# GpSimd left with 64-bit integer additions alone; its float work on VectorE, sums transposed inside PSUM, and a newly planned order

## The chip, the cores and the metric

The kernel runs on one core of one Trainium2 chip. The time is device microseconds from start to end of one launch. The unchanged kernel took 651.06 us (median of three runs, 650.86 to 653.36).

Engine names are those of the profile: PE is TensorE (PEld its weight loads), DVE is VectorE, ACT is ScalarE, POOL is GpSimd, SP is SyncE, which only issues DMAs here.

## The reference

Two attention blocks over separate inputs, S = 2048 tokens, D = 512, 32 heads of 16, bfloat16. Block A is linear attention, block B is full softmax attention. The output holds both side by side.

```python
def _A_ref(x, wqkv, wo):
    ...
    phi = lambda t: jnp.where(t > 0, t + 1, jnp.exp(t)) + 1e-6
    pq, pk = phi(q), phi(k)
    kv = jnp.einsum("bhsd,bhse->bhde", pk, v)
    z = jnp.einsum("bhsd->bhd", pk)
    num = jnp.einsum("bhqd,bhde->bhqe", pq, kv)
    den = jnp.einsum("bhqd,bhd->bhq", pq, z)[..., None] + 1e-6
    o = num / den
    ...
def _B_ref(x, wqkv, wo):
    ...
    scores = jnp.einsum("bhqd,bhkd->bhqk", q, k) * scale
    p = _softmax(scores, axis=-1)
    o = jnp.einsum("bhqk,bhkd->bhqd", p, v)
    return ... @ wo
```

Nearly all the work is in block B: 32 heads x 2048 x 2048 scores, each of which needs an exponential.

## The kernel before, in words

**Blocks and units.** The scores are cut into 2048 blocks of 128 keys x 512 queries of one head. Sixty-four blocks (four heads, which sit on the four 32-row groups `g` of PE, 16 key tiles `j`) make a unit, so there are 32 units `u` = (head group `Gp`, 512 queries `c`, parity `e_`). The products Q K of a block are one matmul (`qk`, L901). Its exponentials P then go into one or three matmuls with V (L1284), which add up in the one PSUM bank `pPV`, four heads on four row groups. The seventeenth column of V is 1.0, so the same matmul gives the sum of the exponentials.

**Two ways to an exponential.** A block goes one of two ways:

- *On ACT* (L1113): two or three blocks, 1024 or 1536 columns, are read from the PSUM tensor `pS` by one `Exp` and written as fp16 to a ring of 25 buffers `PT`. One matmul with V follows per block.
- *On DVE* (L1017, "D blocks"): one `tensor_scalar` reads 512 columns from `pD` (or a spare bank of `pS`) and writes `score*ESC + EB` as int16 into `DI`. The bits of that integer, read as fp16, are a rough exponential. Two more copies of the pattern are made by adding the integers 328 and 656 (`SHIFT`), and three matmuls with V, the first with a scaled V called `VX`, average the three approximations.

**The pattern copies.** Two D blocks (1024 columns) make a group, and there are eight group buffers in `DI`. In the kernel before, POOL makes the two copies as one int32 `tensor_tensor` addition (two int16 values in each 32-bit word, L1208), with up to four copies in one instruction. When POOL is behind, the second copy goes to DVE instead (L1171). POOL also has float work: `VX = VV * 1.55` (L714), the division of a finished unit by its sums (L1319), and a few small ones (L680, L697 to L699).

**The end of a unit.** When `pPV` is complete, DVE transposes it in 32x32 tiles into SBUF (L1313), which frees the bank for the next unit's matmuls. Then come the reciprocal of the sums (L1318, DVE), the product (L1319, POOL) and, after every second unit, a transposition back (L1324, DVE). `last_unit` does the same for the last unit in two halves (L1374 to L1379), and the output projection, the copies to bfloat16 and the stores follow (L1336, L597, L1389).

**What sets the order.** Each engine runs its own list in order. The lists are written by a planner in the kernel's own code: it keeps an estimated clock per engine, estimated durations for every operation and a table `SEG` of weights for each 12 us, and takes the best candidate each time. So a changed duration or weight gives another list on every engine, another choice of which blocks go to ACT and which to DVE, and other merges on POOL. `Sched.add` turns the reads and writes of each operation into semaphore waits. Other work (block A, the projections of block B) is put between as jobs with due times: `bjobs` for block B and for the flag below, `ajobs` for block A.

**The flag.** Row and column norms (`gram_x`, `gram_w`, `flag_job`) tell whether the scores are small enough for this way of taking exponentials. The flag is read at the very end, and a general version in the same program runs only if it is set, which it is not for these inputs.

## Time and profile before

| | |
|---|---|
| median of three runs | 651.06 us |
| profiled execution | 651.69 us |
| span from its first to its last instruction | 649.9 us |
| ACT busy | 633.5 us, 97% |
| PE busy | 637.8 us, 98% |
| DVE busy | 622.5 us, 96% |
| POOL busy | 616.8 us, 95% |
| granted TensorE clock | 0.999 |

The profile describes one execution. A row of a group has the line, engine and operation, what is written from what, the shape and count, then the busy time of the whole group, the mean of one instruction in ns, and the idle time just before them with what ended it. On ACT and DVE one instruction starts before the last has quite ended, so the busy time of a group is less than its count times the mean. A busy share says nothing by itself about which engine sets the end.

### The profile page before, as it was taken

How to read it: one execution, taken by the hardware profiler on the slowest of the kernel's cores; microseconds unless marked ns; L12 is line 12 of the kernel's file. 1: busy time of each engine (PE TensorE's matmuls, PEld its weight loads, DVE VectorE, ACT ScalarE, POOL GpSimd, SP SyncE). 2: the span in 40 equal slices, each digit the busy share in tenths (PEclk: the TensorE clock that was granted, in tenths of full speed). 3: DMA queues.
4: the chain of work that ended last, by engine and by line, in shares of the span. 5: the costliest groups of instructions: out<-in, count | busy, mean ns of one | idle time of the engine just before them, and what ended most of it. 6: DMA issues, size and time to landing. Idle time of an engine off the chain costs nothing.

```text
span 649.9 us, 19218 instructions
## 1 busy us (share of the span) xinstructions
PE 637.8 (98%) x8355; PEld 214.4 (33%) x8356; DVE 622.5 (96%) x1080; ACT 633.5 (97%) x689; POOL 616.8 (95%) x347
## 2 busy tenths in 40 slices
PE   8999999999999999999999999999999999999996
PEld 5333333332333334332232323332223332223332
DVE  4999999999999999999999999999999999999974
ACT  5999999999999999999999999999999999999994
POOL 5899999999999999999999999999999999999950
PEclk9999999999999999999999999999999999999999
DMA  9701000211100110200220200011000001100212
GB/s 171 220 2 24 12 1 10 43 24 29 16 20 2 34 34 2 40 9 7 48 69 2 49 26 19 2 34 42 24 13 22 3 2 42 34 18 17 50 50 69
DMA packets 53224, 21.73 MB, mean 33 GB/s; under 512 B 44176, under 2 KB 52624, under 8 KB 53136
## 3 DMA queue, kind: packets, MB, share of 16 engines
q1 hardware_dynamic: 51664, 19.80, 13.3%
q8 instruction: 67, 1.10, 0.7%
q10 hardware_dynamic: 1472, 0.66, 0.4%
q14 instruction: 21, 0.17, 0.1%
HBM read 4.46 MB, written 4.19 MB: 13 GB/s over the span
## 4 chain that ended last, share of the span: by engine, by line
ACT 66%; PE 16%; DVE 16%; DMA 1%; issue 0%; SPq 0%
ACT PT L1113 65%; DVE DI L1017 11%; PE pPV L1284 5%; PE pS L901 5%; PE pD L611 2%; ACT EA L723 1%; PE pS L611 1%; DVE DI L1171 1%; DMA xTb<-in_B_x_dram 1%; DVE PQT L726 1%; DVE VNa L813 1%; DVE KNa L597 0%; DVE OT L1313 0%; PE pS L1336 0%; PE pD L901 0%; DMA KNa<-VNa 0%
## 5 line engine op out<-in xcount | busy, mean ns | idle before, releaser
L1113 ACT ACTIVATE PT<-pS 128x1024 f16<-128x1024 f32 (+1 forms) x651 | 619.4, 1096 | 1.9 <-PE pS L901 1.0
L1208 POOL TENSOR_TENSOR DI<-DI,CW 128x1024 int32<-128x1024 int32 (+2 forms) x264 | 580.7, 2232 | 5.8 <-DVE DI L1017 4.3
L1017 DVE TENSOR_SCALAR DI<-pD 128x512 int16<-128x512 f32 x512 | 336.9, 682 | 5.7 <-PE pD L901 3.9
L901 PE MATMUL pS<-QT,KM 32*128 32x512 bf16 x1532 | 259.5, 384 | 2.9 <-ACT PT L1113 2.0
L1284 PE MATMUL pPV<-PT,VV 128*17 128x512 f16 x1338 | 232.6, 381 | 0.0
L1284 PE MATMUL pPV<-DI,VV 128*17 128x512 f16 x1420 | 232.0, 382 | 0.1
L901 PE MATMUL pD<-QT,KM 32*128 32x512 bf16 x516 | 185.7, 384 | 0.5 <-DVE DI L1017 0.4
L1284 PE MATMUL pPV<-DI,VX 128*17 128x512 f16 x710 | 162.8, 381 | 0.4 <-DVE OT L1313 0.4
L901 PEld LDWEIGHTS pS<-QT,KM 32*128 32x128 bf16 x1532 | 65.1, 91 | 238.9 <-ACT PT L1113 190.6
L1017 DVE TENSOR_SCALAR DI<-pS 128x512 int16<-128x512 f32 x194 | 131.5, 678 | 0.3 <-PE pS L901 0.3
L1284 PEld LDWEIGHTS pPV<-PT,VV 128*17 128x17 bf16 x1338 | 52.2, 88 | 42.4 <-issue 32.4
L1284 PEld LDWEIGHTS pPV<-DI,VV 128*17 128x17 bf16 x1420 | 49.5, 88 | 45.0 <-issue 33.6
L1171 DVE TENSOR_SCALAR DI<-DI 128x1056 int16<-128x1056 int16 x73 | 49.8, 687 | 0.2
L901 PEld LDWEIGHTS pD<-QT,KM 32*128 32x128 bf16 x516 | 44.2, 91 | 7.6 <-DVE DI L1017 5.2
L1284 PEld LDWEIGHTS pPV<-DI,VX 128*17 128x17 bf16 x710 | 35.6, 88 | 21.8 <-issue 15.7
L611 PE MATMUL pD<-Wa,xTa 128*32 128x256 bf16 x640 | 26.3, 275 | 0.1
L611 PE MATMUL pD<-xTb,Wb 128*32 128x512 bf16 x288 | 23.2, 384 | 0.0
L1313 DVE STREAM_TRANSPOSE OT<-pPV 128x512 f32<-128x512 f32 x31 | 21.9, 706 | 0.0
L1319 POOL TENSOR_TENSOR OT<-OT,ZR 128x256 bf16<-128x256 f32 x31 | 19.3, 621 | 1.1 <-DVE ZR L1318 1.0
L611 PEld LDWEIGHTS pD<-Wa,xTa 128*32 128x32 bf16 x640 | 14.0, 96 | 10.3 <-issue 6.1
L597 DVE CAST KNa<-pD 128x512 bf16<-128x512 f32 x21 | 14.3, 681 | 3.1 <-PE pD L611 3.1
L714 POOL TENSOR_SCALAR VX<-VV 128x544 bf16<-128x544 bf16 x16 | 10.2, 646 | 6.5 <-DVE VV L711 6.5
(139 smaller groups left out, 381.5 us busy)
## 6 DMA issues: line engine op xcount, KB each, us to landing
out_dram<-KNa SPq DMA_DIRECT2D x31, 128.0 KB, 1.7
Wa<-in_A_wqkv_dram SPq DMA_DIRECT2D x1, 1536.0 KB, 8.0
KM<-KR SPq DMA_DIRECT2D x96, 16.0 KB, 1.8
Wb<-in_B_wqkv_dram SPq DMA_DIRECT2D x2, 384.0 KB, 5.7
Wb<-in_B_wqkv_dram SPq DMA_DIRECT2D x1, 512.0 KB, 4.7
Wa<-in_A_wo_dram SPq DMA_DIRECT2D x1, 512.0 KB, 4.3
Wa<-in_B_wo_dram SPq DMA_DIRECT2D x1, 512.0 KB, 3.8
ON<-in_B_x_dram ACTq DMA_DIRECT2D x1, 256.0 KB, 2.9
```

Source lines behind the costliest of these rows:

```text
L597: return lambda e, bk: (e.tensor_copy(out_fn(), in_fn(bk)) if lane == "dve" else e.activation(out_fn(), in_fn(bk), ACTF.Copy))
L611: ins = self.e.matmul(out_[32 * g:32 * g + 32], lhsT=lhsT[:, 32 * g:32 * g + 32], rhs=rhs, start=start, stop=stop, tile_position=(0, 32 * g))
L714: st.append(("pool", 0.61, f_op("pool", lambda e: e.tensor_scalar(VX[:, r, 4 * t4:4 * t4 + 4, :].rearrange("p t c -> p (t c)"), VV[:, r, 4 ...
L723: ("act", 0.0635 + n * 0.000833, f_ev("act", lambda e, bk: e.activation(EA[:, 0:n], f32v(bk)[:, c0:c0 + n], ACTF.Exp), [], ["EA"])),
L901: return e.matmul(dst, lhsT=KM[32 * g:32 * g + 32, Gp % 2, e_, j * 128:(j + 1) * 128], rhs=QT[32 * g:32 * g + 32, Gp % 2, c * 512:(c + 1) ...
L1017: sch.add("dve", lambda e: e.tensor_scalar(DI[:, di_at(0, buf) + i * 512:di_at(0, buf) + (i + n) * 512], f32v(DBANK[b0], n * 512), ESC, EB ...
L1113: sch.add("act", lambda e: e.activation(PTf[:, p0 * 512:p0 * 512 + w], S5[:, c0:c0 + w], ACTF.Exp, scale=SC), reads=skeys(sl, len(bl)), wr ...
L1171: sch.add("dve", lambda e: e.tensor_scalar(gapped(DI, di_at(2, buf), wide // 32, 32), DI[:, di_at(0, buf) - 32:di_at(0, buf) + w], 1.0, fl ...
L1208: sch.add("pool", lambda e: e.tensor_tensor(dv, sv, cv, op=ALU.add), reads=keys + ["CW"], writes=[("DI", v, x) for v in vs for x in best])
L1284: sch.add("pe", lambda e, g=g, j=j, c0=c0, V_=V_, r2=r2, P=P, first=first, last_=last_: e.matmul(PVb[32 * g:32 * g + 17, 0:512] if len(P.s ...
L1313: sch.add("dve", lambda e: e.transpose(OT[:, 0, :], PVb[:, 0:512]), reads=[("PV", g) for g in range(4)], writes=[("OT", 0)])
L1319: ("pool", 0.59, f_op("pool", lambda e: e.tensor_tensor(xn[:, :, 16 * e_:16 * e_ + 16], o[:, :, 0:16], zr.unsqueeze(2).broadcast_to([128, ...
```

## The change

What it does, step by step:

1. **Copies.** Every pattern copy is one `int64_add` on POOL: four int16 values in a 64-bit word, plus a constant that holds 328 or 656 four times. There is one instruction per copy of a group (1024 int16 columns), never both copies in one. None goes to DVE any more; L1171 is gone, and with it its padded place in `DI`, so all rows for the matmuls are contiguous.
2. **Float work.** `VX` (16 instructions), the product of a unit (31 and the two halves of the last), the mask of `gram_w` and the three products of the flag go from POOL to DVE.
3. **End of a unit.** The transposition writes back into `pPV` itself. Reciprocal and product read the bank, so it is free for the next unit only after the product. The queries of Q are stored so that neighbouring ones of two 32-tiles form pairs; the transposition back then moves 4-byte pairs, 256 columns in place of 512.
4. **Start.** POOL writes the ones of V earlier, clears one `DI` pattern and runs one small `int64_add` on it at about its fifteenth instruction. Ahead of that first `int64_add` the built program has an instruction that loads other code for POOL (an `ISA` of line 526).
5. **Order.** New `SEG`, new durations for POOL (`PFX`, `PEL`), other due times: the Q and K projections of later head groups are spread, and the flag's jobs are due from 60 us instead of last.

In the program that results, 721 blocks go to DVE and 1327 to ACT, where there were 710 and 1338. ACT has 615 `Exp` of 1024 columns, 32 of 1536 and one of 512 (before: 615, 36 and none), and 32 of block A as before. DVE's evictions of D blocks are 703 of 512 columns and 9 of 1024 (before: 702 and 4).

The lines of the changed file are shifted: L901 is L912 there, L1017 is L1028, L1113 is L1124, L1284 is L1282, L1313 is L1311, L1318 is L1320, and the product is L1316. L1208 is the copy on POOL in both.

**POOL, around the product of the third unit, before** (sizes of `DI` are in 32-bit words, so 512 words are one copy of a group, 1024 both copies; OT is the product):

```order
L1208 TENSOR_TENSOR DI<-DI,CW 128x1024 x3
L1208 TENSOR_TENSOR DI<-DI,CW 128x512
L1319 TENSOR_TENSOR OT<-OT,ZR 128x16x16
L1208 TENSOR_TENSOR DI<-DI,CW 128x1024 x2
L1208 TENSOR_TENSOR DI<-DI,CW 128x2x512
L1208 TENSOR_TENSOR DI<-DI,CW 128x1024 x2
L1208 TENSOR_TENSOR DI<-DI,CW 128x512
```

The same engine from there to the end, changed:

```order
L1208 ISA DI<-DI 128x512 x30
L1208 ISA DI<-DI 128x2x512 x4
L1208 ISA DI<-DI 128x512 x250
L1208 ISA DI<-DI 128x256 x2
L1208 ISA DI<-DI 128x512 x86
L1208 ISA DI<-DI 128x256 x2
L1208 ISA DI<-DI 128x512 x344
L1208 ISA DI<-DI 128x256 x2
```

The list has become one kind of instruction, 720 of them where there were 264 larger ones, with nothing between.

**DVE, at the end of the seventh unit, before** (from the transposition to the reciprocal; DI from pD or pS are evictions of D blocks, KR a projection of K):

```order
L1313 STREAM_TRANSPOSE OT<-pPV 128x512
L1017 TENSOR_SCALAR DI<-pS 128x512
L1017 TENSOR_SCALAR DI<-pD 128x512
L649 CAST KR<-pD 128x512
L1017 TENSOR_SCALAR DI<-pS 128x512
L1017 TENSOR_SCALAR DI<-pD 128x512 x2
L1017 TENSOR_SCALAR DI<-pS 128x512
L1017 TENSOR_SCALAR DI<-pD 128x512
L1318 RECIPROCAL ZR<-OT 128x16
```

The same place, changed:

```order
L1311 STREAM_TRANSPOSE pPV<-pPV 128x512
L1028 TENSOR_SCALAR DI<-pS 128x512
L1028 TENSOR_SCALAR DI<-pD 128x512
L777 CAST VNa<-pD 128x4x128
L1028 TENSOR_SCALAR DI<-pS 128x512
L1028 TENSOR_SCALAR DI<-pD 128x512
L1320 RECIPROCAL ZR<-pPV 128x16
L1316 TENSOR_TENSOR OT<-pPV,ZR 128x8x2x16
```

Other work still stands between transposition and reciprocal, but now `pPV` is held until the last row. Over the 31 units there are 3.5 such instructions on average between the transposition and the product (0 to 10).

**PE, its last rows, before** (pPV matmuls of the last unit, then the output projection, `Wa` with `ON` and `xTb`):

```order
L1284 MATMUL pPV<-PT,VV 17x512 x12
L611 MATMUL pD<-Wa,ON 32x512 x12
L611 MATMUL pD<-Wa,xTb 32x512 x4
L1336 MATMUL pD<-Wa,ON 128x512 x3
L1336 MATMUL pS<-Wa,ON 128x512 x3
L1336 MATMUL pD<-Wa,xTb 128x512
L1336 MATMUL pS<-Wa,ON 128x512 x3
L1336 MATMUL pS<-Wa,xTb 128x512
L1336 MATMUL pS<-Wa,ON 128x512 x2
L1336 MATMUL pS<-Wa,xTb 128x512
L1336 MATMUL pS<-Wa,ON 128x512
L1336 MATMUL pS<-Wa,xTb 128x512
```

Changed:

```order
L1282 MATMUL pPV<-PT,VV 17x512 x7
L1336 MATMUL pS<-Wa,ON 128x512 x6
L1336 MATMUL pD<-Wa,xTb 128x512 x2
L1336 MATMUL pS<-Wa,xTb 128x512 x2
```

The sixteen L611 matmuls and six of the `ON` ones have gone to earlier places; the four `xTb` ones, which need the last transposition, now stand together at the end.

The diff, cut to its core:

```diff
-    PW = 0.4
+    PW = 0.5
...
-    TEND = 660.0
+    TEND = 632.0
...
-    PFX = 0.144
+    PFX = 0.173
+    PEL = 0.00041
...
-        DI = sb("DI", [128, NDG * (32 + 2 * DGW + (DGW // 32) * 33 + 32)], I16)
-        DIR = 32 + 2 * DGW + (DGW // 32) * 33 + 32
+        DIR = 3 * DGW
+        DI = sb("DI", [128, NDG * DIR], I16)
...
-        DW = DI.bitcast(mybir.dt.int32)
+        DW = DI.bitcast(mybir.dt.uint64)
...
+        sch.add("pool", lambda e: e.memset(DI[:, 0:DGW], 0.0), writes=[("DI", 0, 0, 0)])
+        sch.add("pool", lambda e: e.int64_add(DW[:, 0:8], DW[:, 8:16], 0), reads=[("DI", 0, 0, 0)], writes=[("DI", 0, 0, 0)])
...
+        def paired(ap):
+            return ap.rearrange("p (m t a) -> p m a t", t=32, a=2)
+        def in_pairs(ap):
+            return ap.rearrange("p (m a t) -> p m a t", t=32, a=2)
...
-                st.append(("dve", 0.6, f_ev("dve", lambda e, bk: e.tensor_copy(QT[:, r, cs], f32v(bk)), [], [("QT", r, sc)])))
+                st.append(("dve", 0.6, f_ev("dve", lambda e, bk: e.tensor_copy(in_pairs(QT[:, r, cs]), paired(f32v(bk))), [], [("QT", r, sc)])))
...
-            st.append(("pool", 0.61, f_op("pool", lambda e: e.tensor_scalar(
-                VX[:, r, 4 * t4:4 * t4 + 4, :].rearrange("p t c -> p (t c)"), VV[:, r, 4 * t4:4 * t4 + 4, :].rearrange("p t c -> p (t c)"),
+            st.append(("dve", 0.37, f_op("dve", lambda e: e.tensor_scalar(
+                gapped(VX[:, r, t4, :], 0, 33, 17), VV[:, r, t4, :],
...
-            def on_dve(st_, en_):
-                wide = w + 32
-                sch.add("dve", lambda e: e.tensor_scalar(gapped(DI, di_at(2, buf), wide // 32, 32), DI[:, di_at(0, buf) - 32:di_at(0, buf) + w], 1.0, float(SHIFT[1]),
-                                                         op0=ALU.mult, op1=ALU.add), reads=rk, writes=[("DI", 2, buf)])
-                give(buf, 2, "dve", en_)
...
-                sch.add("pool", lambda e: e.tensor_tensor(dv, sv, cv, op=ALU.add), reads=keys + ["CW"], writes=[("DI", v, x) for v in vs for x in best])
+                for v in vs:
+                    word = int.from_bytes(struct.pack("<4H", *[SHIFT[v - 1]] * 4), "little")
+                    sch.add("pool", lambda e, v=v, word=word: e.int64_add(at64(v), at64(0), word), reads=keys, writes=[("DI", v, x) for x in best])
+                    T["pool"] = st_ = st_ + PFX + len(best) * w * PEL
...
-            if p_backlog(s_["t"]) - DSH * d_backlog(s_["t"]) > PSH:
-                vs = (1,)
-                push("dve", s_["t"], 1, 0.06 + (w + 32) * 0.00053, on_dve)
...
-            sch.add("dve", lambda e: e.transpose(OT[:, 0, :], PVb[:, 0:512]), reads=[("PV", g) for g in range(4)], writes=[("OT", 0)])
-            pvopen[0] = t_ + LPE["dve"]
...
+            sch.add("dve", lambda e: e.transpose(PVb[:, 0:512], PVb[:, 0:512]), reads=[("PV", g) for g in range(4)], writes=[("PV", g) for g in range(4)])
...
+            def scaled(bk):
+                sch.add("dve", lambda e: e.tensor_tensor(xn[:, :, :, 16 * e_:16 * e_ + 16], o[:, :, :, 0:16],
+                                                         zr.unsqueeze(3).broadcast_to([128, 8, 2, 16]), op=ALU.mult),
+                        reads=[("PV", g) for g in range(4)] + [("ZR", 0)], writes=[("XN", xb, e_)])
+                pvopen[0] = T["dve"] + LPE["dve"]
...
-                st.append(("dve", 0.626, f_op("dve", lambda e: e.transpose(on_at(k), XN[:, xb, :]), [("XN", xb, 0), ("XN", xb, 1)], on_keys(k))))
+                st.append(("dve", 0.35, f_op("dve", lambda e: e.transpose(on_at(k).bitcast(U32), XN[:, xb, :].bitcast(U32)), [("XN", xb, 0), ("XN", xb, 1)], on_keys(k))))
...
+        bjobs += [gram_x(i, ready=GR0 + i * GR1) for i in range(4)] + [gram_w(i, ready=GR0 + (4 + i) * GR1) for i in range(2)] + [flag_job(ready=GR0 + 6 * GR1)]
         bjobs.sort(key=lambda j_: j_.ready)
-        bjobs += [gram_x(i, ready=0) for i in range(4)] + [gram_w(i, ready=0) for i in range(2)] + [flag_job(ready=0)]
```

More of the change, by code (lines that the diff above doesn't have):

```diff
@@ L526, in bass_concat_heads__linear_attn_block__softmax_full_mha__prompt_kernel @@
             sch.add("pool", lambda e, r_=r_, e_=e_, sc_=sc_: e.memset(KM[:, r_, e_, sc_ * 512:(sc_ + 1) * 512], 0.0), writes=km_keys(r_, e_, sc_))
-        for r_ in range(2):
-            sch.add("pool", lambda e, r_=r_: e.memset(
-                VV[:, r_, :, :].rearrange("p t (h c) -> p t h c", c=17)[:, :, :, 16:17], 1.0), writes=[("VV1", r_)])
         mk_ident(identf, "identf")
@@ L1182, in on_pool @@
             def on_pool(st_, en_):
-                near_ = {x[1]: x for x in pshift if x[0] == vs and x[2] == w and x[3][0] <= st_ + PMW}
+                near_ = {x[1]: x for x in pshift if x[2] == w and x[3][0] <= st_ + PMW}
                 near_[buf] = me[0]
```

116 lines of the change are left out of this document (56 added, 60 removed), and 108 rows, old and new, of the table SEG.

## The prediction

> **What bounds the kernel now.** First the page's busy shares, which settle nothing:
>
> ```profile
> PE 637.8 (98%) x8355; PEld 214.4 (33%) x8356; DVE 622.5 (96%) x1080; ACT 633.5 (97%) x689; POOL 616.8 (95%) x347
> ```
>
> Then the engines' busy time in one stretch (columns PE, PEld, DVE, ACT, POOL), from ACT's first `Exp` of a block to its last, with the two timeline rows that bound the stretch and the waits of ACT:
>
> ```profile
> 9.02:639.69 630.67, 624.98 (x8247) 205.50 (x8248) 615.55 (x1060) 629.86 (x683) 608.32 (x317) 1.00 0.13 31
> ...
> 9.02 4.62 ACT L1113 ACTIVATE PT<-pS 128x1536 f16<-128x1536 f32 x4 [1.05 <-PE pS L901]
> 634.85 4.84 ACT L1113 ACTIVATE PT<-pS 128x1536 f16<-128x1536 f32 x4
> ...
> ACT PT L1113 <- PE pD L901: 0.7, 1, 0.7
> ```
>
> ACT works 629.86 of 630.67 us. In all that time it stands still for 0.8 us. The other three are idle 6 to 22 us there. So the time is 9.02 us of start, an unbroken stream of exponentials, and 10.2 us after it (649.9 - 639.69). The chain of waits agrees only roughly, as between 344 and 446 us it runs mostly through DVE (pieces with their start and length), with the longest wait of PE behind it:
>
> ```profile
> ACT 66%; PE 16%; DVE 16%; DMA 1%; issue 0%; SPq 0%
> ...
> 344.45 1.88 DVE DI L1017 x3
> ...
> 446.75 56.86 ACT PT L1113 x61
> ...
> PEld pS L901 <- ACT PT L1113: 190.6, 472, 0.9
> ```
>
> There DVE is as full as ACT, but ACT idles no more than the 0.7 us. PE, 98% busy, waits 190.6 us for ACT to free a bank (its weight loads stand and wait, while earlier matmuls count as busy). PE has the most room.
>
> From this follows the rule for the change: work taken off POOL or DVE shortens nothing by itself. It counts only as far as it lets blocks move from ACT to DVE, or shortens the two ends.
>
> **ACT's stream.** Its parts, by shape:
>
> ```profile
> L1113 ACT ACTIVATE PT<-pS 128x1024 f16<-128x1024 f32 x615 | 576.5, 1071 | 0.8 <-PE pD L901 0.7
> L1113 ACT ACTIVATE PT<-pS 128x1536 f16<-128x1536 f32 x36 | 54.7, 1519 | 1.0 <-PE pS L901 1.0
> ```
>
> An `Exp` of 1024 columns costs 576.5/615 = 0.937 us of stream. Each 512 columns more cost 1519 - 1071 = 448 ns, so 1536 cost 1.385 and 512 cost 0.489. The change has four fewer of 1536 and one more of 512: -4 x 1.385 + 0.489 = -5.05 us. Bounds: with 54.7/36 = 1.519 for the wide one, -5.6; with 448 ns for each of the 11 blocks and no start cost, -4.9. I take **-5.0 us**. The 32 block A exponentials stay.
>
> **POOL.** The trace has no 64-bit addition, so its price is bounded by what POOL does now:
>
> ```profile
> L1208 POOL TENSOR_TENSOR DI<-DI,CW 128x2048 int32<-128x2048 int32 x79 | 283.4, 3600 | 1.7 <-DVE DI L1017 0.5
> L1208 POOL TENSOR_TENSOR DI<-DI,CW 128x1024 int32<-128x1024 int32 x132 | 246.9, 1892 | 4.1 <-DVE DI L1017 3.8
> L1208 POOL TENSOR_TENSOR DI<-DI,CW 128x512 int32<-128x512 int32 x53 | 55.0, 1039 | 0.0
> L714 POOL TENSOR_SCALAR VX<-VV 128x544 bf16<-128x544 bf16 x16 | 10.2, 646 | 6.5 <-DVE VV L711 6.5
> L1319 POOL TENSOR_TENSOR OT<-OT,ZR 128x256 bf16<-128x256 f32 x31 | 19.3, 621 | 1.1 <-DVE ZR L1318 1.0
> ```
>
> The two-operand addition costs (1892 - 1039)/512 = 1.67 ns a word and 0.19 us to start. The one-operand row L714 costs (646 - 186)/544 = 0.85 ns an element. One new instruction covers 1024 int16 columns, 256 words of 64 bits, from one operand:
>
> - below: 256 x 0.85 + 186 = 0.40 us;
> - above, as 512 words at the two-operand price: 1.04 us;
> - between: 256 at 1.67, or 512 halves at 0.85, both with 186: 0.61 and 0.62 us.
>
> I take 0.62, since it is one operand (L714's kind) but twice the bytes. The 1442 copies are 721 instructions' worth: 721 x 0.62 = 447 us, where the five rows add up to 615. From 17 us to the end of the stream there are 623 us, so POOL would be busy 72% of it and decides only from 623/721 = 0.86 us an instruction. Its relief is worth nothing directly: PE waited for copies 5.0 us in all, inside the room it has.
>
> ```profile
> PEld pPV L1284 <- POOL DI L1208: 5.0, 20, 0.4
> PEld pPV L1284 <- DVE OT L1313: 1.8, 5, 0.5
> ```
>
> **DVE.** The rows that carry the balance:
>
> ```profile
> L1171 DVE TENSOR_SCALAR DI<-DI 128x1056 int16<-128x1056 int16 x73 | 49.8, 687 | 0.2
> L1017 DVE TENSOR_SCALAR DI<-pD 128x512 int16<-128x512 f32 x508 | 332.1, 678 | 5.7 <-PE pD L901 3.9 <-PE pS L901 1.1
> L1313 DVE STREAM_TRANSPOSE OT<-pPV 128x512 f32<-128x512 f32 x31 | 21.9, 706 | 0.0
> L1318 DVE RECIPROCAL ZR<-OT 128x16 f32<-128x16 f32 x31 | 7.4, 238 | 0.0
> L724 DVE TENSOR_SCALAR EC<-EA 128x528 bf16<-128x528 bf16 x32 | 13.4, 418 | 0.5 <-ACT EA L723 0.3
> L1324 DVE STREAM_TRANSPOSE ON<-OT 128x512 bf16<-128x512 bf16 x12 | 8.4, 702 | 0.0
> L1374 DVE STREAM_TRANSPOSE OT<-pPV 128x256 f32<-128x256 f32 x2 | 0.8, 425 | 0.8 <-PE pPV L1284 0.8
> L1428 DVE TENSOR_SCALAR KM<-pD,PAR 128x256 bf16<-128x256 f32 x2 | 0.9, 474 | 0.0
> ```
>
> Off: the 73 copies, 49.8 us. On: 16 `VX` like L724's gapped rows, 16 x 0.43 = 6.9; 31 products of 256 columns from PSUM like L1428, 31 x 0.47 = 14.7 (0.42 at least, by L724); 11 more D blocks at 332.1/508 = 0.65, 7.2; the flag's small ones, about 1. The 15 transpositions back fall from 702 to some 425 ns (L1374 has 256 columns of 4 bytes): -4.2. The transposition into PSUM is not in the trace; I price it as L1313 (no less than L1374's 425, and twice 706 would add 22 us, which is all that DVE gains). Sum: -24 us, so DVE falls to about 598 us. That hides under ACT's stream, and would still if the transposition doubled (620).
>
> **The bank held longer.** Before, `pPV` was closed for one transposition, 0.71 us. Now it is closed for the transposition, the 3.5 instructions that stand between on average (3.5 x 0.65 = 2.3), the reciprocal 0.24 and the product 0.47: about 3.7 us, 31 times. Behind the waiting pPV matmul on PE stand the next Q K matmuls, for which ACT waits. Its cover is the order: the planner has put Q K matmuls and projections there, and the 190.6 us that PE waits for ACT at present, 0.4 us each time. Meanwhile ACT fills 2 x 3.7/0.937 = 8 of its 25 buffers. I cost it, with all other gaps that a new order brings, at **+0.7 us** of idle ACT, about what it has now on top of the old; between -0.8 (all old gaps gone) and +5 (0.16 us a unit).
>
> **The start.** ACT's first `Exp` hangs on the first tokens' DMA, which stays. POOL's own start, now and at its first copy:
>
> ```profile
> 8.87 0.24 POOL L532 MEMSET VNa<- 128x32 bf16 x1
> ...
> 17.02 1.89 POOL L1208 TENSOR_TENSOR DI<-DI,CW 128x1024 int32<-128x1024 int32 x1 [1.39 <-DVE DI L1017]
> ```
>
> POOL is through at 9.1 us and has its first copy at 17.0. The new clearing and small addition put about 1 us on it, like the 1039 ns of a 512-word row, so loading the new code may last 7 us before anything is late. No row here shows such a load. The Trainium skill, "GPSIMD Engine Reference", section "2.1 Instruction dispatch", says that the first call of a freshly loaded kernel pays about 6 us more. By that POOL would be ready near 16 us, within the 17.0, and the sum stays.
>
> **The end.** From the last `Exp` to the last copy:
>
> ```profile
> 640.72 0.45 DVE L1374 STREAM_TRANSPOSE OT<-pPV 128x256 f32<-128x256 f32 x1 [0.80 <-PE pPV L1284]
> 641.48 0.40 POOL L1376 TENSOR_TENSOR OT<-OT,ZR 128x128 bf16<-128x128 f32 x1 [2.24 <-DVE ZR L1375]
> 642.87 0.42 DVE L1379 STREAM_TRANSPOSE xTb<-OT 128x256 bf16<-128x256 bf16 x1
> 644.72 0.38 PE L1336 MATMUL pS<-Wa,xTb 128*128 128x512 bf16 x1
> 645.13 0.69 DVE L597 CAST KNa<-pS 128x512 bf16<-128x512 f32 x1 [0.39 <-PE pS L1336]
> ```
>
> From 640.72 to 643.29 the two halves overlap between DVE and POOL. The same on DVE alone is twice (0.42 + 0.20 + 0.35 + 0.25) = 2.4 us (the last two terms estimates from POOL's 0.40 and from half of 0.42, rounded up), so 0.2 less. From there the last copy starts 1.84 us later now, as eight matmuls of the output projection are still in PE's queue. In the change only four are, and DVE has one other copy first (0.65): 1.2 less. I take **-1.4 us** (0 to -2).
>
> **The sum.** 649.9 - 5.0 - 1.4 + 0.7 = 644.2 us of span. The profiled execution took 1.8 us more than its span (651.69), which gives 646.0; the median of the runs is 0.6 below that execution, so **645.4 us**, 0.9% faster. With the bounds of the terms, 642.4 (-5.6, -2, -0.8) to 651.1 (-4.9, 0, +5).
>
> **Rivals.**
>
> - *Equal: new gaps eat the gain.* The order is new everywhere, and 4 to 6 us of idle ACT in place of 0.8 give 649 to 651. For it: ACT waits on nothing now, so every new gap is a loss. Against: DVE and POOL both get 24 us or more of room. 12%.
> - *Slower: the held bank.* If PE has too little to do while `pPV` is closed, each unit stops the stream. From 0.2 us of ACT per unit (6 us over 31) the gain is gone; with 0.5 it is 15.5 - 6.4 = 9 us more than before, 660. For it: PE already waited for L1313 with 0.71 us of closing. Against: the matmuls that the order has put there. 7%.
> - *Slower: 64-bit additions at the upper price.* At 1.04 us POOL needs 750 us from 17 us on, and with 10 us of end and 1.2 outside the span it is 778. 4%.
> - *Code load not hidden.* A load far over 7 us makes the first copies late and PE stops in order behind them. At 12 us the first copies are 5 us late, 650. No row here speaks for so long a load, and none excludes it. 3%. By the page's 6 us it would not come to this.
> - *Faster than forecast.* If ACT's own instructions run closer together when its banks come sooner: the last two rows of the stream are 4.84 us for four, against 2 x (0.937 + 1.385) = 4.64, so some slack exists; 0.5% of the stream is 3 us, 642. 4%.
>
> **How the numbers follow.** The forecast has 70%. About half a per cent, 3.3 us, is what a measurement of this kernel can tell from no change. Faster by more (under 647.8): nearly all of the forecast (66%), the last rival (4%), 2% of the first. Slower by more (over 654.3): the held bank and the 64-bit price, and part of the load, 13%. The rest, 15%, is no change. The likeliest case's own range is 642.4 to 649; the range of 8 in 10 reaches over the equal case, 642.5 to 652.
>
> **What would show it.** Right: ACT busy about 5 us less in an unbroken stream, POOL near 0.6 us per copy and 70%, DVE near 598 us, 3.7 us (now 5.1) from the first half's transposition to the end of the last copy. Wrong: ACT idle with pPV or L1208 ahead of it, POOL above 95%, a copy late at 17 us, or a stream shorter than 623 us.

## The result and the profile after

The changed kernel took **661.15 us** (median of four runs, 660.22 to 661.88); the kernel before took 651.03 us in the same session. The ratio is 1.0146, with a 95% interval of 1.012 to 1.0173. The forecast was 645.4 us, so the change made slower what it was forecast to make faster.

The span of the profiled execution grew by 9.8 us, from 649.9 to 659.7. The two rows that bound `ScalarE`'s stream of exponentials split it: the start is 6.1 us longer (15.13 instead of 9.02), the stream 5.2 us longer (635.83 instead of 630.67), and the end 1.4 us shorter (8.8 from the last `Exp`, instead of 10.2).

**The stream.** Busy time by engine in stretches of the changed kernel (columns: stretch, its length, PE, PEld, DVE, ACT, POOL with their instructions, granted clock, DMA share, GB/s): the whole stream, then 5.3, 5 and 5 us in its middle.

```profile
15.14:650.97 635.83, 624.02 (x8296) 205.12 (x8296) 600.48 (x1042) 628.00 (x680) 436.62 (x735) 0.99 0.12 29
...
314.70:320.00 5.30, 4.30 (x76) 1.60 (x68) 3.19 (x6) 5.04 (x6) 3.29 (x6) 1.00 0.09 20
320.00:325.00 5.00, 2.43 (x17) 0.48 (x17) 3.50 (x7) 0.00 (x0) 1.20 (x2) 0.70 0.11 25
325.00:330.00 5.00, 5.00 (x50) 0.93 (x46) 3.29 (x6) 3.39 (x4) 1.72 (x4) 0.62 0.11 27
```

ACT is idle 7.8 us in the stream (635.83 - 628.00), where it had been 0.8. Nearly all of it is one standstill: from 320 to 325 us ACT does nothing at all. Note the clock beside it: 1.00 ahead of the standstill, 0.70 in it and 0.62 behind it, when PE is full again. The loss goes on after its cause has gone.

The chain of waits of that stretch gives the cause (start, length, what; SPq is the issuing of a transfer by SyncE):

```profile
314.30 0.61 DVE KR L660
...
318.65 0.59 SPq L665
319.24 0.04 issue
319.28 1.84 DMA KM<-KR
321.12 0.04 DVEq L111
321.15 0.04 issue
321.20 0.69 DVE KR L660
```

`KR` is the buffer from which a K projection is spread into `KM` by eight transfers (L665). There are two such buffers. In the new order three projections of head group 2 are cast at 314.2, 316.0 and 321.2 us; the third has to wait until the eight transfers of the first, which SyncE starts one after another, have read its buffer. In the kernel before, the casts of that group stood at 271.5, 288.8, 307.4 and 319.6 us. Who waited for it on PE (us, times, longest):

```profile
PE pD L912 <- DVE KR L660: 2.9, 1, 2.9
```

The cast empties a bank of `pD`, so the next scores wait for it on PE. Then the matmuls with V wait another 0.6 us for the unit's product on DVE: the cast stands between the transposition at 312.4 us and the product at 322.7, so `pPV` is held meanwhile. ACT waits for the scores behind all this, 5.5 us in one piece.

**The start.** The timeline of the first 20 us of the changed kernel (start, length, engine, instruction, idle time before it and who ended it):

```profile
9.10 0.28 POOL L497 TENSOR_SCALAR_AFFINE_SELECT identb<-identb 128x128 bf16<-128x128 bf16 x1 [8.09 <-issue]
19.59 0.19 POOL L526 INT64_ADD DI<-DI  x1 [7.09 <-issue]
...
9.44 1.03 PE L1408 MATMUL pS<-identb,ON 128*128 128x128 bf16 x8 [5.00 <-POOL ZMk L514]
...
10.51 0.60 ACT L608 ACTIVATE xTb<-pS 128x512 bf16<-128x512 bf16 x1 [6.65 <-PE pS L1408]
15.13 2.36 ACT L1124 ACTIVATE PT<-pS 128x1536 f16<-128x1536 f32 x2 [2.11 <-PE pS L912]
```

GpSimd stands still twice without waiting for anything that the profile shows: 8.1 us ahead of its first affine select, and 7.1 us ahead of the small 64-bit addition. The first makes the identity that PE needs at L1408. In the kernel before the same step waited 0.24 us:

```profile
1.24 0.29 POOL L494 TENSOR_SCALAR_AFFINE_SELECT identb<-identb 128x128 bf16<-128x128 bf16 x1 [0.24 <-POOL identb L493]
```

Ahead of each standstill the program has a pair of instructions that change GpSimd's code (POOLq is its sequencer; shortest, median and longest in ns, then first and last start in us):

```profile
L497 POOLq MODIFY_POOL_CONFIG  x2: 11/11/11, 1.2 to 1.3; - x2
L526 POOLq MODIFY_POOL_CONFIG  x2: 11/11/11, 12.7 to 12.7; - x2
```

The kernel before has the first pair alone, at L494 and also at 1.2 us, and does not stand still behind it. So the program asks for one set of code ahead of its first affine select and for another ahead of the 64-bit addition.

**The rest** is near the forecast. Groups of the changed kernel (busy, mean ns of one, idle before):

```profile
L1208 POOL INT64_ADD DI<-DI x720 | 431.4, 612 | 192.9 <-DVE DI L1028 190.7
L1311 DVE STREAM_TRANSPOSE pPV<-pPV 128x512 f32<-128x512 f32 x31 | 22.4, 721 | 0.0
L1316 DVE TENSOR_TENSOR OT<-pPV,ZR 128x256 bf16<-128x256 f32 x31 | 13.8, 445 | 1.1
```

So the theory after the result was: two losses, apart in time, hide a gain. **A**: GpSimd holds one set of code, each execution starts with the set that the one before it left, and asking for the other one costs a load. **C**: two buffers are too few for three K projections close together. Rivals are named with each experiment.

### The profile page after: what moved, and what is told of

Same layout as the page of the kernel before. It is cut to its first block, busy times and chain, and to the rows that moved or that the text cites. A ratio compares the mean times of both kernels' runs of the same rounds, so it can differ in the third digit from the quotient of the medians.

```text
span 659.7 us, 19641 instructions
## 1 busy us (share of the span) xinstructions
PE 635.9 (96%) x8376; PEld 213.4 (32%) x8378; DVE 607.4 (92%) x1063; ACT 631.7 (96%) x686; POOL 440.2 (67%) x750
## 4 chain that ended last, share of the span: by engine, by line
PE 63%; DVE 19%; ACT 14%; issue 2%; SPq 1%; DMA 1%; POOL 0%; POOLq 0%; DVEq 0%
PE pPV L1282 24%; PE pS L912 21%; ACT PT L1124 14%; DVE DI L1028 12%; PE pD L622 7%; PE pS L622 4%; DVE pPV L1311 1%; PE pD L718 1%; PE pD L912 1%; PE pS L718 1%; DVE OT L1316 1%; PE pD L675 1%; SPq L665 1%; DMA KM<-KR 1%; DVE EC L735 1%
## 5 line engine op out<-in xcount | busy, mean ns | idle before, releaser
L1124 ACT ACTIVATE PT<-pS 128x1024 f16<-128x1024 f32 (+1 forms) x648 | 617.2, 1078 | 9.9 <-PE pD L912 6.0
L1208 POOL INT64_ADD DI<-DI x720 | 431.4, 612 | 192.9 <-DVE DI L1028 190.7
L1028 DVE TENSOR_SCALAR DI<-pD 128x512 int16<-128x512 f32 (+1 forms) x503 | 336.5, 690 | 21.4 <-PE pD L912 16.0
L912 PE MATMUL pS<-QT,KM 32*128 32x512 bf16 x1536 | 259.4, 386 | 2.7 <-ACT PT L1124 2.3
L1282 PE MATMUL pPV<-PT,VV 128*17 128x512 f16 x1327 | 236.3, 383 | 0.4 <-DVE OT L1316 0.4
L1282 PE MATMUL pPV<-DI,VV 128*17 128x512 f16 x1442 | 230.9, 384 | 0.1
L912 PE MATMUL pD<-QT,KM 32*128 32x512 bf16 x512 | 177.4, 387 | 3.1 <-DVE KR L660 2.9
L1282 PE MATMUL pPV<-DI,VX 128*17 128x512 f16 x721 | 163.3, 385 | 2.0 <-DVE OT L1316 1.9
L1028 DVE TENSOR_SCALAR DI<-pS 128x512 int16<-128x512 f32 x209 | 141.7, 678 | 1.6 <-PE pS L912 1.0
L912 PEld LDWEIGHTS pS<-QT,KM 32*128 32x128 bf16 x1536 | 65.9, 91 | 237.7 <-ACT PT L1124 184.3
L1282 PEld LDWEIGHTS pPV<-PT,VV 128*17 128x17 bf16 x1327 | 50.8, 88 | 42.5 <-issue 33.1
L1282 PEld LDWEIGHTS pPV<-DI,VV 128*17 128x17 bf16 x1442 | 51.0, 88 | 41.5 <-issue 29.1
L912 PEld LDWEIGHTS pD<-QT,KM 32*128 32x128 bf16 x512 | 42.7, 91 | 8.4 <-DVE KR L660 3.2
L1282 PEld LDWEIGHTS pPV<-DI,VX 128*17 128x17 bf16 x721 | 36.5, 89 | 26.4 <-issue 14.5
L622 PE MATMUL pD<-Wa,xTa 128*32 128x256 bf16 x800 | 33.7, 275 | 0.9 <-DVE DI L1028 0.6
L1311 DVE STREAM_TRANSPOSE pPV<-pPV 128x512 f32<-128x512 f32 x31 | 22.4, 721 | 0.0
L622 PE MATMUL pS<-xTb,Wb 128*32 128x512 bf16 x208 | 16.3, 384 | 0.4 <-DVE DI L1028 0.2
L1316 DVE TENSOR_TENSOR OT<-pPV,ZR 128x256 bf16<-128x256 f32 x31 | 13.8, 445 | 1.1
L735 DVE TENSOR_SCALAR EC<-EA 128x528 bf16<-128x528 bf16 x32 | 13.4, 420 | 0.1
```

The source lines that it names most:

```text
L622: ins = self.e.matmul(out_[32 * g:32 * g + 32], lhsT=lhsT[:, 32 * g:32 * g + 32], rhs=rhs, start=start, stop=stop, tile_position=(0, 32 * g))
L735: ("dve", 0.06 + n * 0.00054, f_op("dve", lambda e: e.tensor_scalar(gapped(EC, 0, n // 16 + 1, 16), EA[:, 0:n + 16], 1.0, 1e-6, op0=ALU.mi ...
L912: return e.matmul(dst, lhsT=KM[32 * g:32 * g + 32, Gp % 2, e_, j * 128:(j + 1) * 128], rhs=QT[32 * g:32 * g + 32, Gp % 2, c * 512:(c + 1) ...
L1028: sch.add("dve", lambda e: e.tensor_scalar(DI[:, di_at(0, buf) + i * 512:di_at(0, buf) + (i + n) * 512], f32v(DBANK[b0], n * 512), ESC, EB ...
L1124: sch.add("act", lambda e: e.activation(PTf[:, p0 * 512:p0 * 512 + w], S5[:, c0:c0 + w], ACTF.Exp, scale=SC), reads=skeys(sl, len(bl)), wr ...
L1208: sch.add("pool", lambda e, v=v, word=word: e.int64_add(at64(v), at64(0), word), reads=keys, writes=[("DI", v, x) for x in best])
```

## The experiments

"Both repairs" below is the changed kernel with the first two edits together (e3). The kernel before, run again beside the experiments, took 651.0 to 651.3 us in the median each time.

### One code set

The small 64-bit addition (and the clearing of the words that it reads) becomes GpSimd's first instruction. The affine selects behind it then need no load of their own, which the order of the changed kernel had shown: behind L526 the identity in float32 and `BMk` are made without a pause.

```diff
+        sch.add("pool", lambda e: e.memset(DI[:, 0:64], 0.0), ...)
+        sch.add("pool", lambda e: e.int64_add(DW[:, 0:8], DW[:, 8:16], 0), ...)
         mk_ident(identb, "identb")
...
-        sch.add("pool", lambda e: e.memset(DI[:, 0:DGW], 0.0), ...)
-        sch.add("pool", lambda e: e.int64_add(DW[:, 0:8], DW[:, 8:16], 0), ...)
```

> The changed kernel with one edit: the first two instructions on GpSimd are now a small memset of DI and the small 64-bit addition, ahead of the identity that L497 makes, and their old place at L526 is empty. Nothing else moves. Theory A (GpSimd keeps one set of code, the set with the 64-bit addition also holds the affine select, and each execution of the changed kernel finds the set that the one before it left: so it loads twice, 8.1 us ahead of L497 and 7.1 us ahead of L526): nothing is loaded now, the first affine select waits under 1 us, the first Exp begins at 9 to 10 us and not at 15.1, and the time falls by 5 to 6.5 us to about 655. Theory B (the first 64-bit addition of an execution costs its load in any case): the load stands ahead of the identity, the first Exp is no earlier than about 14.5 us and the time stays at 660 to 661.5.

Measured (e1): 655.17 us (654.82 to 656.47), 6.0 less than the change. Timeline of its start, and the one request for code that is left:

```profile
1.09 0.20 POOL L502 INT64_ADD DI<-DI  x1
...
1.60 0.29 POOL L497 TENSOR_SCALAR_AFFINE_SELECT identb<-identb 128x128 bf16<-128x128 bf16 x1 [0.16 <-POOL identb L496]
...
8.89 8.72 ACT L1124 ACTIVATE PT<-pS 128x1536 f16<-128x1536 f32 x8 [1.05 <-PE pS L912]
...
L502 POOLq MODIFY_POOL_CONFIG  x2: 11/11/11, 1.0 to 1.0; - x2
```

Theory A stands: nothing is loaded, not even ahead of the first 64-bit addition, so the set was there from the execution before; theory B is out. The runs e5 and e10 below test it once more. The Trainium skill, "GPSIMD Engine Reference", section "2.1 Instruction dispatch", has the load at about 6 us with the first call after loading; here it took 8.1 and 7.1 us at the start of the changed kernel, and that it comes back with every execution that ends with the other set is what the runs add.

### Four buffers

```diff
-            kr = krc[0] % 2
+            kr = krc[0] % 4
+            KRk = KR[:, kr, :] if kr < 2 else OTb[:, 0, (kr - 2) * 512:(kr - 1) * 512]
...
```

> The changed kernel with one edit: the K projections of head groups 1 to 3 are cast into four buffers in turn, not two (the two new ones lie in the half of OT that the change left empty). The order of every engine is the same. Theory C (the standstill at 319.7 to 329 us is the third cast of a close group of three at L660, which waits until the eight transfers of the first have read its buffer, behind which the evictions, the scores and ScalarE stand): no gap above 1 us between Exps is left there, the clock stays near 1, and the time falls by 5.5 to 7 us to about 654.5. Theory D (the transfers of three projections in a row hold back the scores that read KM, whatever the number of buffers, since SyncE starts them 0.66 us apart): a gap of at least 4 us stays between 314 and 335 us and the time falls by less than 2.5 us.

Measured (e2): 655.25 us (654.76 to 655.78), 5.9 less than the change. The same three stretches:

```profile
314.70:320.00 5.30, 4.84 (x81) 1.76 (x78) 5.27 (x11) 4.53 (x6) 2.89 (x6) 1.00 0.09 22
320.00:325.00 5.00, 5.00 (x69) 1.40 (x65) 4.97 (x9) 4.49 (x5) 3.94 (x7) 1.00 0.11 27
325.00:330.00 5.00, 5.00 (x66) 1.50 (x63) 4.60 (x8) 5.00 (x6) 4.51 (x9) 1.00 0.11 27
```

The standstill is gone, and the clock stays at 1.00. One gap of 1.2 us is left, a little over what theory C allowed; theory D had asked for 4. The stream is 630.2 us now.

### Both

> Both edits: the 64-bit addition ahead of the identity, and four buffers for the K projections. If theories A and C hold and the two losses are apart in time, they add up: 661.2 - 6 - 6.5, about 648.5 (647 to 650), below the kernel before at 651.0 by 0.2 to 0.6%. If the first Exp's gain is given back later (ScalarE then waits for tokens or keys where it now finds them ready), or the standstill only moves to the next wait, the time stays at 652 or more.

Measured (e3): **649.46 us** (649.17 to 649.73); against the kernel before 0.9969, interval 0.9956 to 0.9981. The gains add up (6.0 + 5.9 = 11.9; measured 11.7). This version beats both kernels, by 0.3% and 1.8%. Busy shares on its page:

```profile
PE 632.0 (98%) x8378; PEld 211.9 (33%) x8378; DVE 606.9 (94%) x1063; ACT 631.6 (97%) x686; POOL 440.3 (68%) x750
```

And its stream, in the columns of above:

```profile
9.28:639.42 630.14, 621.69 (x8298) 204.75 (x8296) 600.36 (x1042) 627.93 (x680) 432.46 (x722) 1.00 0.13 31
```

Its span is 648.0, though, and the forecast was 644.2: 3.8 us are still to be told.

### The bank freed early

The forecast had named the held bank as a rival. In the changed kernel PE waits 10.8 us for the product at the unit's end (`PEld pPV L1282 <- DVE OT L1316`, 8.5 us, and 2.3 us more as `PE`), so the next experiment took the hold away, on top of the one code set.

```diff
-            sch.add("dve", lambda e: e.transpose(PVb[:, 0:512], PVb[:, 0:512]), ...)
-            o = PVb[:, 0:512].rearrange(...)
+            sch.add("dve", lambda e: e.transpose(OT[:, 0, :], PVb[:, 0:512]), ...)
+            o = OT[:, 0, :].rearrange(...)
...
```

> e1_one_code_set with one more edit: the transposition at the end of a unit writes OT, as in the kernel before, not its own PSUM bank, so that the next unit's first PV product waits for one VectorE instruction and not for four (transposition, reciprocal and the two products). Every engine's order stays, and the standstill at the K projections stays too. Theory E (the held bank is what spreads small delays over ScalarE's row: its records are 3 us longer than the number of Exps explains): the waits of TensorE for the unit end fall from 10.8 us to under 3 us, and the time falls by 1.5 to 3.5 us against e1's 655.2, to about 652.5. Theory F (those waits are filled with scores that are ahead of ScalarE, so the held bank is free): under 0.8 us, 654.4 to 656.

Measured (e4): 660.39 us (659.24 to 661.09), 5.2 us **more** than without the edit. Both theories missed. The waits of PE went as expected:

```profile
PEld pPV L1282 <- DVE OT L1311: 0.2, 1, 0.2
```

Something else came. The product's line in that run, with its shortest, median and longest duration in ns:

```profile
L1316 DVE TENSOR_TENSOR OT<-OT,ZR x31: 439/804/830, 38.0 to 634.7; 128x256 bf16<-128x256 f32 x31
```

The product has both its operands in SBUF now, and takes 0.80 us in the median instead of 0.445. Of the 31, the eleven that took 0.439 to 0.451 us had next to no GpSimd addition beside them (55 ns at most), and the eighteen of 0.80 us and more had 0.5 to 0.83 us of one. Of the two between, that of 0.64 had 0.35 us of one, and that of 0.46 had one beside it from end to end, an exception that stays unexplained. In the version with the operand in PSUM the products took 0.436 to 0.457 us, though for 19 of the 31 an addition ran beside them from end to end. So this is contention of VectorE with GpSimd, and the transposition within the bank avoids it. The Trainium skill, "SBUF — State Buffer", section "SBUF: two separate sides", says that an instruction of VectorE with two SBUF inputs and one of GpSimd that reads SBUF exclude each other from a shared port; the trace agrees but for the one exception, 0.80 against 0.44.

> e4_bank_freed_early with spare buffers for the K projections of head group 2 (two places of ON that are empty at that time, since OT is in use again): all three repairs on the changed kernel's order. If the three losses are independent, e4's time less 5.7 us: by theory E 646.5 to 648.5, by theory F the same as e3_both, 649 to 650. Over 651 would mean that the early bank and the spare buffers bring the next wait forward.

Measured (e9): 655.28 us (655.05 to 655.9): 5.1 less than the run before, as the spare buffers should give, and 5.8 more than both repairs alone. With the standstill out of the way the early bank loses about the same. The spare buffers were worth 5.7 us with the bank held (e1 to e3), so the hold adds little to the standstill, some 0.6 us.

### What VectorE's time and the held bank cost

Two runs on top of both repairs add one short reciprocal per unit, once behind the product and once ahead of it.

```diff
+                sch.add("dve", lambda e: e.reciprocal(ZR[:, 1, 0:16], ZR[:, 0, 0:16]), ...)
```

> e3_both with one more VectorE instruction per unit, a reciprocal of the 16 reciprocals into a spare place (some 0.24 us, 31 times, 7.4 us in all), put behind the product at the end of a unit, where the PSUM bank is already free. It prices VectorE's time at that place, which e4_bank_freed_early raised by 6.8 us. Theory H (VectorE at 94% is on the path: what it does at the unit end delays the evictions and, behind them, the scores): e3's 649.5 rises by 4 to 8 us, to 653.5 to 657.5, and e4's loss is told by VectorE's time alone. Theory I (VectorE has slack and e4 lost by something else): 649 to 651.

> The same extra reciprocal, put ahead of the product, so that the unit's PSUM bank is held 0.24 us longer besides: e12_recip_after and this one differ only in how long the next unit's first PV product waits. Theory J (the hold is filled with scores that are ahead of ScalarE): within 1 us of e12. Theory K (the hold is on the path): slower than e12 by 0.1 to 0.24 us for each of the units, 3 to 7 us.

Measured: 651.06 us (650.61 to 651.99) behind (e12), 652.9 us (652.57 to 653.39) ahead (e15). Their streams, in the columns of above:

```profile
8.51:639.68 631.17, 622.70 (x8298) 205.42 (x8296) 601.95 (x1073) 628.73 (x680) 433.02 (x724) 1.00 0.13 31
8.77:641.78 633.01, 622.98 (x8298) 204.86 (x8296) 603.15 (x1073) 629.40 (x680) 432.05 (x723) 1.00 0.13 31
```

Behind, the time is 1.6 us above both repairs, at the upper end of theory I (651) and below all that theory H allowed. Each record is 241 ns, yet in a row with others the 31 added only 1.6 us to DVE's busy time (608.5, from 606.9). Not all of the 1.6 us of time lies in the kernel's own instructions: the span, in the median of the executions, rose by 0.8 (647.7 to 648.5); the rest fell outside it, and why stays open.

Ahead, the time from the reciprocal's start to the product's end grew from 0.720 to 0.826 us per unit, 3.3 us in all, and the run took 1.84 us more than e12, between theories J and K. That would be 0.56 us for each us of hold. But DVE was also busy for 1.2 us more (603.15 against 601.95), so the two runs differ in more than the hold, and 0.56 is the most that it can have cost.

The last run takes the evictions out of the hold: reciprocal and product follow the transposition at once.

```diff
+            sch.add("dve", lambda e: e.reciprocal(zr, o[:, :, :, 16]), ...)
+            sch.add("dve", lambda e: e.tensor_tensor(xn[...], o[...], zr..., op=ALU.mult), ...)
             def scaled(bk):
-                sch.add("dve", lambda e: e.tensor_tensor(xn[...], o[...], zr..., op=ALU.mult), ...)
                 pvopen[0] = T["dve"] + LPE["dve"]
-            st = [("dve", 0.157, f_op("dve", lambda e: e.reciprocal(zr, o[:, :, :, 16]), ...)),
+            st = [("dve", 0.157, lambda bk: None),
```

> e3_both with the reciprocal and the product at the end of each unit put right behind the transposition on VectorE. In e3_both none to ten other VectorE instructions, mostly evictions, stand between the transposition and the reciprocal (0.03 to 5.9 us, about 2 us on average), and for all that time the unit's PSUM bank is held. Nothing else is moved, TensorE's order stays. From e12 and e15 one us of longer hold cost 0.56 us, and the waits of TensorE for the product are 10.4 us. Theory K (the held bank is what is left between e3_both and the forecast): those waits fall to under 5 us and the time falls by 1 to 4 us, to 645.5 to 648.5. Theory L (the evictions that now come 0.7 us later at each unit cost as much): 649 to 652.

Measured (e13): 669.51 us (668.22 to 669.84), 20.1 us more than both repairs. Waits of this version:

```profile
ACT PT L1126 <- PE pS L914: 12.5, 23, 1.3
...
ACT PT L1126 <- PE pD L914: 6.7, 13, 0.8
...
PEld pPV L1284 <- DVE OT L1318: 1.1, 2, 0.9
```

The hold is gone (1.1 us of waits), and ACT now waits 19.2 us for scores, where it was 2.5. What stands next on DVE, mostly an eviction, comes 0.71 us later at each of the 31 units (1.39 us behind the start of the transposition, where it was 0.68 in the mean), 22 us in sum, and PE's own waits for evictions are 15.9 us, where they were 1.8. So the 20 us are, by these waits, the price of the later evictions. Theory K's forecast fails, and L's was far too low. Whatever the hold itself costs, the evictions that this order puts ahead of the reciprocal have less than 0.7 us to spare.

### The parts of the change alone

The 64-bit additions alone, in the old order, with the float work left on GpSimd:

> One part of the change alone: the kernel before, with its own order, its two copies per instruction and its float work on GpSimd, where each 32-bit tensor addition at L1208 is replaced by 64-bit additions of a constant, one for each copy, and a small one ahead of the identity, so that one set of code serves. GpSimd's busy time should fall from 88% to some 71%. Theory of the prediction (the Exps of ScalarE are a closed row, and GpSimd is not the bound, so its relief is worth nothing until the order uses it): the time stays within 0.4% of the kernel before, 649.5 to 652.5. Rival (late copies are what holds back the scores or the PV products of the kernel before): the time falls by 2 us or more, below 649.

Measured (e5): **1121.4 us** (1119.1 to 1122.6). Both theories missed. Waits of GpSimd:

```profile
POOL DI L1216 <- issue: 225.9, 38, 6.3
POOL DI L1216 <- DVE DI L1020: 143.7, 97, 5.8
POOL OT L1327 <- issue: 128.0, 18, 7.5
...
POOL VX L717 <- issue: 70.1, 10, 7.3
```

Each float product between two 64-bit additions seems to load one set and then the other. A run with just three such products put back shows it by itself:

> e3_both with three of VectorE's 16 VX products (the first of head groups 1 to 3, 0.44 us each) put back on GpSimd, between its 64-bit additions, and nothing else. Theory G (from e5_64bit_alone: the float product and the 64-bit addition are in different code sets, and each change of kind loads one): six loads, each 5.5 to 8.5 us of GpSimd's time with issue as the releaser, 33 to 51 us in all, in which copies come late; the time rises by 10 to 40 us to 660 to 690. Rival (the long waits of e5 came from its order, GpSimd waiting for VectorE): GpSimd waits under 5 us at L727 in all, and the time stays at 649 to 651.

Measured (e11): 682.86 us, 33.4 more than both repairs (one run). Timeline of GpSimd around the second and third product:

```profile
197.22 0.68 POOL L727 TENSOR_SCALAR VX<-VV 128x561 bf16<-128x561 bf16 x1 [6.99 <-issue]
203.76 8.24 POOL L1210 INT64_ADD DI<-DI  x14 [5.86 <-issue]
...
399.97 0.68 POOL L727 TENSOR_SCALAR VX<-VV 128x561 bf16<-128x561 bf16 x1 [7.10 <-issue]
406.44 3.54 POOL L1210 INT64_ADD DI<-DI  x6 [5.79 <-issue]
```

Seven us to the float set, 5.8 us back, six loads of 39 us together, and ACT stands still 11.3, 11.1 and 7.7 us behind them. Theory G stands. "GpSimd does only 64-bit additions" is thus no matter of balance: a float instruction that stands alone between such additions takes some 13 us of GpSimd's time (7.1 + 5.8), and each of the three cost 11 us of the kernel's.

The 64-bit additions and the moved float work together, in the old order:

> The new split of the work with the old order: e5_64bit_alone with all float work of GpSimd (16 VX products, 33 unit-end products, the small ones of the flag) on VectorE at the same places, so that GpSimd needs one code set and loads none. Its transposition writes OT as before, so its unit-end products read SBUF alone and can collide with GpSimd. VectorE gets about 16 x 0.44 + 33 x 0.67 = 29 us more than its 622. Theory H (VectorE is on the path as soon as it is fuller): 657 to 680, so the new order and the transposition in the bank are what makes the split pay. Rival (the old order hides it, ScalarE stays the bound): 650 to 653. Below 649 would mean that late copies were a cost in the kernel before.

Measured (e10): 666.74 us (666.43 to 667.13), 15.7 more than the kernel before. The chain of that run (that of the kernel before stands in the prediction), and the copies that are still on DVE:

```profile
DVE 76%; PE 17%; ACT 4%; DMA 1%; issue 1%; ACTq 0%; DVEq 0%; SPq 0%
...
L1174 DVE TENSOR_SCALAR DI<-DI 128x1056 int16<-128x1056 int16 x73 | 49.5, 683 | 0.2
```

VectorE took 18.6 us more (641.1 from 622.5) and the end came 15.7 us later, though ACT had as many blocks and GpSimd far less to do (360.4 us, from 616.8). Theory H stands in that VectorE is on the path as soon as it is fuller. That the split needs the new order is not shown: the 73 copies, which the change takes off VectorE, are still there in this run, and its products at the unit's end read SBUF alone, eleven of the 31 taking 0.47 to 1.2 us and the others 0.40 to 0.43.

The two runs also test theory A. They open alike, but GpSimd's last instruction is a float product in e5 and a 64-bit addition in e10. The first 64-bit addition of each:

```profile
8.01 0.19 POOL L500 INT64_ADD DI<-DI  x1 [7.07 <-issue]
...
1.09 0.20 POOL L500 INT64_ADD DI<-DI  x1
```

After an execution that ended on a float product the first addition waits 7.1 us, and after one that ended on an addition it waits for nothing.

And the price of the addition, 32-bit in place of 64-bit in the repaired version:

> e3_both, with each 64-bit addition at L1208 replaced by a 32-bit tensor addition of the same 1024 bytes per partition (no second code set at all). It prices the 64-bit addition against the 32-bit one in the same order. From the kernel before, a 32-bit addition of 512 words took 1.88 us, half of it, for the 256 words of one copy, about 1.0 us: 720 additions by 1.0 are 720 us and not 440, so GpSimd becomes the bound and the time is 735 to 780. If the copies were late by less than their buffers hide, or the single copy costs less than half a pair, it is below 700.

Measured (e6): 764.3 us (764.25 to 764.39), 114.9 more than both repairs. Its group and its chain:

```profile
L1213 POOL TENSOR_TENSOR DI<-DI,CW 128x512 int32<-128x512 int32 (+1 forms) x720 | 718.8, 1039 | 24.7 <-DVE DI L1031 24.5
...
POOL 82%; PE 9%; DVE 7%; DMA 1%; issue 0%; ACT 0%
```

In a row one 32-bit addition takes 718.8/720 = 1.00 us, and one 64-bit addition 431.4/720 = 0.60, for the same 2048 bytes per partition (512 words of 32 bits, 256 of 64; the sizes in the expectation are half of the real ones). With 32 bits GpSimd is the bound, as the prediction's rival at the upper price had it.

## Why the prediction was wrong

It was forecast that the time would fall by 0.9%; it rose by 1.5%. Two terms of the sum failed: the +0.7 us for all gaps that the new order brings, which measured +10.0, and the start, "the sum stays", which measured +6.1. (The sum of the prediction's own bounds is 642.7 to 651.2, not 642.4 to 651.1; that changes nothing.) Step by step:

- **ACT's content, -5.0: right.** With the usual spacing of an `Exp`'s start to the next one's (0.904, 1.331 and 0.477 us for 1024, 1536 and 512 columns, the lower quartile in the trace), the content falls from 615, 36 and 32 of them to 615, 32 and 33: -4.85 us.
- **The end, -1.4: right in sum, in part by luck.** From the first half's transposition to the end of the last copy it was 4.05 us, where 3.7 was forecast and 5.1 measured before. The rest came from places that the forecast left alone: that transposition starts 0.55 us earlier behind the last `Exp`, and 0.2 us was lost behind the last copy.
- **The new gaps, +0.7: wrong, +10.0.** What the stream has beyond that content was 11.5 us and is 21.5. Of this 7.0 is idle time, nearly all the standstill at `KR`, and 3.0 is spread over the spacing. The step that failed is the claim that the planner's order covers the gaps. The planner knows the transfers' length, but not that a cast waits for the buffer of two projections earlier, and the order of the change puts three together. The closing of `pPV` itself was as forecast, 3.5 us per unit where 3.7 was taken. The trace of before could not show this wait, the order of the change could: three casts close together beside eight transfers each. I had compared the order on GpSimd, at the unit's end and in the last rows, not there.
- **The start, "the sum stays": wrong, +6.1.** I looked for the load where the change adds the 64-bit addition, found GpSimd idle there up to 17 us, and counted one load of at most 7 us as hidden. That load, 7.1 us, was hidden indeed: with both loads gone the stream of e1 was no shorter (636.2 us against 635.8). The one that cost is the other one: ahead of its first affine select the program asks for a different set, which the 64-bit work of the execution before had driven out. The rival "code load not hidden", at 3%, had the wrong place, the first copies, and not the identity that all of the start hangs on.
- **GpSimd: right.** 0.612 us was measured and 0.62 taken; 67% of the span. The choice between 0.40 and 1.04 rested on an argument that no row tested, so the hit is in part luck. That GpSimd's relief is worth nothing directly fits PE's waits for copies, 5.0 us before and 4.5 in the change. No run tests it alone: e5 loads code all the time, and e10 fills VectorE in the same stroke.
- **DVE, -24: right in records, not in time.** The lengths of DVE's records fall by 25.6 us in sum (701.7 to 676.2), but its busy time by 15.2, to 607.4 instead of 598. Records overlap their neighbours, and a record's length is more than it takes of the engine; e12 shows that for 241 ns records that cost 0.05 us.
- **"That hides under ACT's stream": wrong as a rule.** DVE was counted as slack because its total lies below ACT's. In the runs half of VectorE's time or more came back where an instruction stood ahead of evictions: +1.6 us of busy time cost 0.8 of span (e12), +5.9 cost 5.2 (e4), +18.6 cost 15.7 (e10), and in e13 evictions put off by 22 us in sum cost 20.1, though DVE's busy time rose by 6.4 only. Had the transposition doubled, the forecast would, by these prices, have been further off still.
- **The held bank, 7%: not what made the change slower.** PE waited 10.8 us for it, but made longer it cost 0.56 us per us at most (e15), and the two runs that took it away lost time (e4, e13). These two made evictions later in the same stroke, so what the hold costs by itself is not shown.

With the two losses repaired, 648.0 us of span stand against 644.2. The start is 0.3 longer and the end 0.2 shorter than forecast; the rest is the stream. There ACT is idle 1.4 us more than before (one gap of 1.2 us at the K projections), and the spread-out spacing is 2.9 us more, where the forecast had 0.7 for the two together. What the spacing hangs on stays open.

## What to carry to other kernels

A code set is paid for at each change of kind, and the step from the end of one execution to the start of the next is such a change too: let the first GpSimd instruction use the set that the last one used, and do not mix the two kinds in between. In an order written out by a planner, compare what the planner does not know (how many buffers a step has, and how long its transfers hold them) at every place where the new order brings instances of a step close together. An engine below 100% is no cover: ask how late its next eviction may come, not how much of its total is free.

## What the runs showed of the hardware

- GpSimd's 64-bit addition and its float instructions need different code sets. A change to the set that the float instructions or the first affine select ask for took 7.0 to 8.1 us (e11, the changed kernel), the way back 5.8 to 5.9 us in mid-run (e11) and 7.1 us at the start. Asking for the set that is there costs no wait (e1), and the set stays from one execution to the next (e1; e5 against e10). Behind a 64-bit addition clearings and affine selects ran without a load (e1).
- The 64-bit addition of 256 words per partition took 0.612 us (0.60 in a row), a 32-bit two-operand addition of the same bytes 1.00 us in a row (e6).
- VectorE's product of 256 columns took 0.44 us with one operand in PSUM, whatever GpSimd did, and 0.80 us or more with both in SBUF beside a GpSimd addition in 18 of 20 cases (e4).
- VectorE transposed 128x512 float32 in place in PSUM in 0.721 us, against 0.706 us from PSUM to SBUF.
- After a standstill of some 5 us the granted clock stayed at 0.62 for the next 5 us, while PE was full.
